# Attention scores as (64,32) tiles of the array, and another order of the first loads, in a fused attention and FFN kernel

## The chip, the cores and the metric

The kernel runs on one core of a Trainium2 chip. The metric is the device time of one execution in microseconds (us). TensorE is called PE, VectorE DVE, ScalarE ACT, GpSimd POOL and SyncE SP, as in the profile; PEld is PE's loading of weights.

## The reference

The inputs are q, k and v of 8 batches, 12 heads, 448 positions and 64 elements, two vectors g_q and g_k of 64, and the weights w1, w2 (768 x 1024), w3 (1024 x 1024) and w_out (1024 x 768), all in float32.

```python
q_n, k_n = rmsnorm(q, g_q), rmsnorm(k, g_k)      # x / sqrt(mean(x*x) + 1e-6) * g
scores = q_n @ k_n^T / sqrt(64)
attn = softmax(scores)
x = (attn @ v), as 3584 tokens x 768             # heads side by side
out = ((x @ w1) * (x @ w2)) @ w3 @ w_out
```

## The kernel before

**Units of work.** A quad is four heads of one batch, so there are 24 quads, three to a batch. The 448 positions stand as 112 partitions times J = 4. For each quad, q and k are loaded in float32 by SP (`load_qk`, L98; for quad 0 in two halves, k's on ACT's queue) and v in bfloat16 by POOL (`load_v`, L116).

**Preparation of a quad**, in two halves of two heads (pr = 0, 1): squares on ACT (`prep_sq`, L148), sums on DVE (`prep_red`, L163), the factor alpha = 1/rms by a logarithm and an exponential on ACT (`prep_alpha`, L170), three multiplications on DVE (`prep_scale`, L181): q by alpha, that by the product of both g vectors (`g_b`, L195), k by alpha. Then q and k are transposed to qkT, where the 64 elements of one head stand on partitions 0 to 63 and those of the other on 64 to 127: for quads 0 to 4 on PE, with a copy on DVE (`prep_pe_transpose`, L214), later by a DMA from SP (L210).

**Scores.** `qk_exp(i, g)` (L226) makes two groups of keys, jk, for one half of a quad. For each it issues two matmuls, one for each head, u = 0 and 1: 112 keys as weights, 64 rows, 448 queries moving. Both write one `sc` tile (one PSUM bank each), and one exponential on ACT takes both. The pool of `sc` has two buffers.

**The rest of attention.** `pv_set` (L248) runs three times for a quad: the sums of P over the keys (kind 0, weights of ones), and P times v in two halves. Four heads are four tiles of 32 columns of the array. ACT makes the reciprocal, DVE the product, into xT.

**FFN.** w3 and w_out are multiplied once to w34: 8 transposes of w3 (`w3_transpose`, L290) and 16 units of 8 matmuls (`w34_unit`, L298), 8 for each half nh of w_out's columns. LAG (L64) says how many units later the second half's units begin. `ffn1_a`, `ffn1_b` and `ffn2` (L323 to L374) do x·w1, x·w2 and the product with w34; each group of matmuls is cut in four tiles of 32 columns (`narrow`, L312).

**Order.** The order is written out by hand. A slot t = 4i + sl holds, on every engine in this sequence: loads of q and k that are due, `qk_exp(i, sl)`, one `pv_set` of the quad before (for sl below 3), up to four weight loads from the list wq, one or two pieces of w34 (W34_SLOTS, slots 1 to 13) or, later, up to two pieces of FFN, then the transposes and the other parts of preparation that are due. PREP_1 (L66) and PREP (L70) give, in slots before the quad's own, when each part is due; PREP_1 is for quad 1. What is left of FFN runs after the last slot. Engines work in their own order, so an instruction that waits holds what follows it on its engine.

**The start.** POOL first loads g_q and g_k, each copied to 112 partitions (L401, L402), and makes the identity; then a copy of one column of quad 0's k (`gate`, L410) holds POOL until that k has landed. After it come the loads of w_out's first half (nh = 0), four chunks of w3, v of quad 0, and w_out's second half. The rest of w3, v of quads 1 and 2, w1 and w2 follow from wq. SP is given q and k of quad 0, then of quad 1 (L408) and, in slot 0, of quad 2. PE warms up on 16 matmuls of zeros. DVE multiplies the two g tiles and scales them by 8 to g_b (L424, L425) between alpha and the first scaling.

Of the kernel before, what the change touches and what calls it, by code (L numbers as in the profile page):

```python
# [8 lines left out]
FP = mybir.dt.float32  # L9
BF = mybir.dt.bfloat16  # L10
MULT = mybir.AluOpType.mult
# [7 lines left out]
def kernel(  # L19
# [13 lines left out]
    nc = tc.nc  # L33

    B, H, S, D = q.shape
    NP = 112
    J = S // NP
# [23 lines left out]
    N_PE_T = 5  # L61
    N_SQ_ACT = 24
    W34_EV = "DA"
    LAG = 4  # L64
    SHIFT = [0, 0, 0, -1, -2, -3, -4]
    PREP_1 = {  # L66
        "sq0": -4, "red0": -4, "sq1": -4, "red1": -3, "alpha": -3,
        "sc0": -3, "t0": -2, "sc1": -2, "t1": -1,
    }
    PREP = {  # L70
        "load": -8, "sq0": -5, "red0": -5, "sq1": -4, "red1": -4, "alpha": -3,
        "sc0": -3, "t0": -2, "sc1": -2, "t1": -1,
# [6 lines left out]
    w_outs = const.tile([128, CF, DM], BF, name="w_outs")  # L79
    w3s = big_pool.tile([128, CF, DFF], BF, tag="big", name="w3s")  # L80
    w3T = big_pool.tile([128, CF, DFF], BF, tag="big", name="w3T")
    gq_b = const.tile([NP, D], FP, name="gq_b")
    gk_b = const.tile([NP, D], FP, name="gk_b")
    g_b = const.tile([NP, D], BF, name="g_b")
    ident = const.tile([128, 128], BF, name="ident")
    ones = const.tile([NP, HALF], BF, name="ones")
# [11 lines left out]
    def load_qk(i, split=1, k_eng=None):  # L98
        b, m = divmod(i, NQB)
        s = st[i]  # L100
        s["q"] = load_pool.tile([NP, HQ, J, D], FP, tag="q", name="q_sb")
        s["k"] = load_pool.tile([NP, HQ, J, D], FP, tag="k", name="k_sb")
        n = HQ // split
        for h0 in range(0, HQ, n):
            for t_sb, src, eng in (
                (s["q"], q, nc.sync),
                (s["k"], k, k_eng or nc.sync),
            ):
                eng.dma_start(
                    out=t_sb[:, h0 : h0 + n].rearrange("p h j d -> p h (j d)"),  # L110
                    in_=src[b, HQ * m + h0 : HQ * m + h0 + n].rearrange(
                        "h (p j) d -> p h (j d)", j=J
                    ),
                )

    def load_v(i):  # L116
        b, m = divmod(i, NQB)
        s = st[i]
        s["v"] = load_pool.tile([NP, HQ, J, D], BF, tag="v", name="v_sb", bufs=4)
        nc.gpsimd.dma_start(  # L120
            out=s["v"].rearrange("p h j d -> p h (j d)"),
            in_=v[b, HQ * m : HQ * (m + 1)].rearrange("h (p j) d -> p h (j d)", j=J),
        )
# [9 lines left out]
    def load_w3(c):  # L133
        nc.gpsimd.dma_start(
            out=w3s[:, c, :],
            in_=moe_w3.rearrange("(c p) f -> p c f", p=128)[:, c, :],
        )

    def load_wout(nh, c):
        nc.gpsimd.dma_start(  # L140
            out=w_outs[:, 4 * c : 4 * c + 4, nh * NH : (nh + 1) * NH],
            in_=moe_w_out.rearrange("(c p) n -> p c n", p=128)[
                :, 4 * c : 4 * c + 4, nh * NH : (nh + 1) * NH
            ],
        )


    def prep_sq(i, pr, on_act=False):  # L148
# [77 lines left out]
    def qk_exp(i, g):  # L226
        s = st[i]
        if g == 0:
            s["P"] = att_pool.tile([NP, HQ, J, S], BF, tag="P", name="P")
        pr, t = divmod(g, 2)  # L230
        qkT, P = s["qkT"], s["P"]
        for jk in (2 * t, 2 * t + 1):
            sc = sc_psum.tile([NP, 2, 512], FP, tag="sc", name="sc")
            for u in range(2):
                nc.tensor.matmul(  # L235
                    out=sc[:, u, 0:S],
                    lhsT=qkT[u * D : (u + 1) * D, pr, J + jk, :],
                    rhs=qkT[u * D : (u + 1) * D, pr, 0:J, :].rearrange(
                        "d j p -> d (j p)"
                    ),  # L240
                    start=True,
                    stop=True,
                )
            nc.scalar.activation(  # L244
                out=P[:, 2 * pr : 2 * pr + 2, jk, :], in_=sc[:, :, 0:S], func=AF.Exp
            )
# [151 lines left out]

    with tc.manual_schedule():

        nc.gpsimd.dma_start(out=gq_b, in_=g_q.unsqueeze(0).broadcast_to([NP, D]))  # L401
        nc.gpsimd.dma_start(out=gk_b, in_=g_k.unsqueeze(0).broadcast_to([NP, D]))  # L402
        nc.vector.memset(warm_t, 0.0)
        nc.vector.memset(eps_t, 64e-6)
        nc.vector.memset(ones, 1.0)
        load_qk(0, split=2, k_eng=nc.scalar)
        nc.scalar.preload_act_table_set("natural_log_exp_and_others")
        load_qk(1)  # L408
        make_identity(nc, ident)
        nc.gpsimd.tensor_copy(out=gate, in_=st[0]["k"][:, HQ - 1, 0, 0:1])  # L410
        load_wout(0, 0)
        load_wout(0, 1)
        for c in range(4):
            load_w3(c)
        load_v(0)
        load_wout(1, 0)
        load_wout(1, 1)
        warm(16)
        for pr in range(2):
            prep_sq(0, pr, on_act=True)  # L420
            prep_red(0, pr)
            prep_alpha(0, 2 * pr, 2 * pr + 2)
            if pr == 0:
                nc.vector.tensor_tensor(out=gq_b, in0=gq_b, in1=gk_b, op=MULT)  # L424
                nc.vector.tensor_scalar(  # L425
                    out=g_b, in0=gq_b, scalar1=8.0, scalar2=None, op0=MULT
                )
            prep_scale(0, pr, pe=True)
            if pr == 0:
                prep_pe_transpose(0, 0)  # L430

        wq = [lambda c=c: load_w3(c) for c in range(4, CF)]
        wq.insert(2, lambda: load_v(1))
        wq.append(lambda: load_v(2))
        for h in range(HQ):
            for half in range(2):
                for w, src in ((w1s, moe_w1), (w2s, moe_w2)):
                    wq.append(
                        lambda w=w, src=src, h=h, half=half: load_w12(w, src, h, half)
                    )  # L440
        wq.append(lambda: load_v(3))

        w34q = [lambda: w3_transpose(0), lambda: w3_transpose(1)]
        for fc in range(CF + LAG):
            if fc < CF:
                w34q.append(lambda fc=fc: w34_unit(fc, 0))
            if fc + 2 < CF:
                w34q.append(lambda fc=fc: w3_transpose(fc + 2))
            if fc >= LAG:
                w34q.append(lambda fc=fc: w34_unit(fc - LAG, 1))  # L450

        def prep_part(n, part):
            pe = n < N_PE_T
            if part[:2] == "sq":
                prep_sq(n, int(part[2]), on_act=n < N_SQ_ACT)
            elif part[:3] == "red":
                prep_red(n, int(part[3]))
            elif part == "alpha":
                prep_alpha(n)
            elif part[:2] == "sc":  # L460
                prep_scale(n, int(part[2]), pe=pe)
            elif pe:
                prep_pe_transpose(n, int(part[1]))


        agenda = {}
        for n in range(1, NQ):
            shift = SHIFT[min(n, len(SHIFT)) - 1]
            table = PREP_1 if n == 1 else PREP
            for part, rel in table.items():  # L470
                agenda.setdefault(max(0, 4 * n + rel + shift), []).append((n, part))

        for i in range(NQ + 1):
            for sl in range(4):
                t = 4 * i + sl
                mine = agenda.pop(t, [])
                for n, part in mine:
                    if part == "load":
                        load_qk(n)
                if i < NQ:  # L480
                    qk_exp(i, sl)
                if t == 0:
                    prep_pe_transpose(0, 1)
                seen = len(fillers)
                if i > 0 and sl < 3:
                    pv_set(i - 1, sl)
                fresh = fillers[seen:]
                if sl == 0 and 4 <= i + 1 < NQ:
                    load_v(i + 1)
                for _ in range(4):  # L490
                    if wq:
                        wq.pop(0)()
                if t in W34_SLOTS:
                    for _ in range(W34_SLOTS[t]):
                        if w34q:
                            w34q.pop(0)()
                elif not w34q:
                    left = (14 - t) % 12 + 1
                    old = len(fillers) - sum(1 for f in fillers if f in fresh)
                    fill(min(2, -(-old // left)))  # L500
                for n, part in mine:
                    if part[0] == "t":
                        prep_part(n, part)
                for n, part in mine:
                    if part[0] != "t" and part != "load":
                        prep_part(n, part)
        fill(len(fillers))
# [28 lines left out]
```

## Time and profile before

| | us |
|---|---|
| median of 13 runs | 392.55 |
| lowest, highest | 391.14, 393.98 |
| the profiled execution's own time | 391.63 |
| its span, first to last instruction | 389.9 |
| first scores (slot 0) start | 13.30 |
| first w3 transpose starts | 20.96 |
| first DMA of w_out is issued | 6.61 |

The profile is of one execution. A row of a group gives busy time and the mean length of one instruction; matmuls overlap, since the next one starts before the one before has left the array, so the distance between starts tells more than the length. In the timeline each row is a run of equal instructions: start, time until the last end, engine, line, names, and in brackets the idle time ahead of it with what ended it. The granted PE clock was full in the span but for the stretch from 11 to 25 us, where it was half.

### The profile page before, as it was taken

What the parts mean: (1) busy time and instruction counts of PE and PEld (TensorE: products, weight loads), DVE (VectorE), ACT (ScalarE), POOL (GpSimd) and SP (SyncE); (2) the same over time, 40 slices, a digit from 0 to 9 for tenths busy, and PEclk for the clock granted to TensorE, in tenths of its full rate; (3) what the DMA queues carried; (4) which work ended last, traced back from release to release, by engine and by line L of the source; (5) the groups of instructions that cost most, each with busy time, mean ns of one, the idle gap of its engine ahead of it and who ended that gap; (6) DMA issues with size and microseconds to landing.
All of it is one profiled execution on the core that took longest, in us unless ns stands there. A gap on an engine that the chain in (4) does not pass through costs nothing.

```text
span 389.9 us, 14802 instructions
## 1 busy us (share of the span) xinstructions
PE 372.3 (96%) x6688; PEld 193.3 (50%) x6688; DVE 242.2 (62%) x383; ACT 285.2 (73%) x467; POOL 35.4 (9%) x61
## 2 busy tenths in 40 slices
PE   5489999999999999999999999999999999999995
PEld 1155554544544455445544554445445555456563
DVE  1766766887767577567766766757776672234232
ACT  4559889998888885897899768888889857751210
POOL 5232440000000000000000000000000000000000
PEclk9579999999999999999999999999999999999999
DMA  8999999476994589675877479558955652003014
GB/s 186 226 236 237 222 227 180 69 148 141 217 190 88 114 168 208 127 162 95 189 174 151 86 221 204 76 109 199 205 92 122 119 141 27 3 12 114 2 26 141
DMA packets 78367, 55.08 MB, mean 141 GB/s; under 512 B 37824, under 2 KB 72160, under 8 KB 78304
## 3 DMA queue, kind: packets, MB, share of 16 engines
q1 hardware_dynamic: 61568, 41.30, 44.4%
q0 software_dynamic: 16256, 12.38, 22.4%
q8 instruction: 52, 0.85, 0.9%
q10 hardware_dynamic: 480, 0.46, 0.4%
q14 instruction: 11, 0.09, 0.1%
HBM read 46.72 MB, written 11.01 MB: 148 GB/s over the span
## 4 chain that ended last, share of the span: by engine, by line
PE 87%; DMA 8%; ACT 1%; DVE 1%; POOL 0%; issue 0%; ACTq 0%
PE pa L314 19%; PE po L314 19%; PE pb L314 19%; PE pv L259 15%; PE sc L235 12%; DMA w3s<-in_moe_w_dram 4%; PE wps L301 3%; DMA w_outs<-in_moe_w_out_dram 3%; DMA k_sb<-in_k_dram 1%; PE w3T_ps L293 1%; PE qkT_ps L220 0%; ACT P L244 0%; DVE qtmp L188 0%; ACT w34s L286 0%; DVE qks L201 0%; ACT sq L157 0%
## 5 line engine op out<-in xcount | busy, mean ns | idle before, releaser
L244 ACT ACTIVATE P<-sc 112x896 bf16<-112x896 f32 x192 | 165.5, 916 | 42.1 <-PE sc L235 42.1
L344 DVE TENSOR_TENSOR abT<-pb,a_sb 128x448 bf16<-128x448 f32 x64 | 40.0, 624 | 77.1 <-PE pb L314 56.7
L314 PE MATMUL pa<-xT,w1s 128*32 128x448 bf16 x1536 | 84.0, 353 | 0.0
L314 PE MATMUL pb<-xT,w2s 128*32 128x448 bf16 x1536 | 83.8, 352 | 0.0
L314 PE MATMUL po<-w34s,abT 128*32 128x384 bf16 x1792 | 77.9, 326 | 0.0
L166 DVE TENSOR_REDUCE ssq<-sq 112x16 f32<-112x1024 f32 x48 | 58.3, 1215 | 14.2 <-ACT sq L157 14.2
L314 PEld LDWEIGHTS <-abT 128*32 128x32 bf16 x1792 | 47.3, 97 | 27.6 <-issue 2.4
L235 PE MATMUL sc<-qkT 64*112 64x448 bf16 x384 | 57.4, 378 | 0.7 <-DVE qkT L223 0.7
L314 PEld LDWEIGHTS <-w2s 128*32 128x32 bf16 x1536 | 41.2, 97 | 31.4
L314 PEld LDWEIGHTS <-w1s 128*32 128x32 bf16 x1536 | 39.8, 96 | 34.0 <-issue 4.7
L331 ACT CAST a_sb<-pa 128x448 bf16<-128x448 f32 x64 | 34.0, 531 | 26.5 <-PE pa L314 26.5
L363 DVE COPY o_sb<-po 128x384 f32<-128x384 f32 x56 | 31.2, 557 | 31.5 <-PE po L314 31.5
L259 PE MATMUL pv<-P,v_sb 112*32 112x448 bf16 x768 | 45.1, 355 | 0.0
L120 POOL DMA_DIRECT2D v_sb<-in_v_dram x24 | 17.0, 709 | 237.6 <-PE pv L259 217.6
L188 DVE TENSOR_TENSOR qtmp<-q_sb,alpha 112x512 bf16<-112x512 f32 x48 | 32.7, 682 | 5.7 <-ACT alpha L177 5.7
L235 PEld LDWEIGHTS <-qkT 64*112 64x112 bf16 x384 | 17.5, 126 | 31.8 <-issue 29.4
L201 DVE TENSOR_TENSOR qks<-k_sb,alpha 112x512 bf16<-112x512 f32 x48 | 32.8, 684 | 0.0
L157 ACT ACTIVATE sq<-q_sb 112x512 f32<-112x512 f32 x48 | 30.5, 635 | 1.8 <-DMA q_sb<-in_q_dram 1.8
L275 DVE TENSOR_TENSOR xT<-pv,r 128x448 bf16<-128x448 f32 x48 | 29.6, 616 | 3.2 <-PE pv L259 3.2
L157 ACT ACTIVATE sq<-k_sb 112x512 f32<-112x512 f32 x48 | 30.0, 625 | 0.0
L259 PEld LDWEIGHTS <-v_sb 112*32 112x32 bf16 x768 | 16.2, 95 | 23.6 <-issue 15.1
L301 PE MATMUL wps<-w_outs,w3T 128*128 128x384 bf16 x128 | 23.4, 332 | 0.0
(36 smaller groups left out, 174.1 us busy)
## 6 DMA issues: line engine op xcount, KB each, us to landing
q_sb<-in_q_dram SPq DMA_DIRECT2D x23, 448.0 KB, 5.6
k_sb<-in_k_dram SPq DMA_DIRECT2D x23, 448.0 KB, 6.2
v_sb<-in_v_dram POOLq DMA_DIRECT2D x24, 224.0 KB, 4.7
out_dram<-o_sb SPq DMA_DIRECT2D x8, 336.0 KB, 4.0
out_dram<-o_sb SPq DMA_DIRECT2D x8, 288.0 KB, 3.4
w3s<-in_moe_w_dram POOLq DMA_DIRECT2D x8, 256.0 KB, 15.0
out_dram<-o_sb SPq DMA_DIRECT2D x8, 240.0 KB, 4.4
w_outs<-in_moe_w_out_dram POOLq DMA_DIRECT2D x4, 384.0 KB, 13.4
```

Of the source, the lines that this page charges most:

```text
L157: nc.scalar.activation(out=sq[:, t], in_=src[:, hs], func=AF.Square)
L166: nc.vector.tensor_reduce(out=s["ssq"][:, :, hs, :], in_=s.pop(("sq", pr)), axis=AX, op=ADD)
L188: nc.vector.tensor_tensor(out=qtmp.transpose([0, 2, 1, 3]), in0=s["q"][:, hs], in1=alpha[:, 0, hs].unsqueeze(3).broadcast_to([NP, 2, J, D] ...
L201: nc.vector.tensor_tensor(out=qks[:, 1].transpose([0, 2, 1, 3]), in0=s["k"][:, hs], in1=alpha[:, 1, hs].unsqueeze(3).broadcast_to([NP, 2, ...
L235: nc.tensor.matmul(out=sc[:, u, 0:S], lhsT=qkT[u * D : (u + 1) * D, pr, J + jk, :], rhs=qkT[u * D : (u + 1) * D, pr, 0:J, :].rearrange("d ...
L244: nc.scalar.activation(out=P[:, 2 * pr : 2 * pr + 2, jk, :], in_=sc[:, :, 0:S], func=AF.Exp)
L259: nc.tensor.matmul(out=ps[h * HALF : (h + 1) * HALF, :], lhsT=w, rhs=P[:, h, jk, :], start=(jk == 0), stop=(jk == J - 1), tile_position=(0 ...
L301: nc.tensor.matmul(out=ps[:, 0:NH], lhsT=w3T[:, gc, fc * 128 : (fc + 1) * 128], rhs=w_outs[:, gc, nh * NH : (nh + 1) * NH], start=(gc == 0 ...
L314: nc.tensor.matmul(out=ps[32 * h : 32 * h + 32, 0:n], lhsT=lhsT[:, 32 * h : 32 * h + 32], rhs=rhs, start=start, stop=stop, tile_position=( ...
L331: nc.scalar.copy(out=a_sb, in_=ps[:, 0:S])
L344: nc.vector.tensor_tensor(out=abT[bp][:, fi, odd * S : (odd + 1) * S], in0=ps[:, 0:S], in1=a_tiles.pop((b, fi)), op=MULT,)
L363: nc.vector.tensor_copy(out=o_sb[:, nh * NH : (nh + 1) * NH], in_=ps[:, 0:NH])
```

## The change

Six things are changed.

- The scores: each matmul with 112 keys as weights becomes four, with 32, 32, 32 and 16 keys, each at its own 32 columns of the array and the 64 rows of its head.
- The g vectors: each is loaded as one row of 64 by ACT's queue, after quad 0's k. DVE makes 8·g_q·g_k in one instruction, PE spreads it to 112 partitions (a matmul with a row of ones), and DVE copies it to g_b.
- The loads of weights: the gate on POOL is gone, so they are issued after the identity. Their order is another: w_out's second half (o1) comes after the last chunk of w3.
- Quad 1's q and k are loaded in slot 0 in place of ahead of it.
- Quad 1's preparation is due one slot later, part for part.
- LAG is 8 in place of 4: the units of w34 for w_out's second half come after all those for the first.

That five quads are transposed on PE (N_PE_T) is so in both.

```diff
-    LAG = 4
+    LAG = 8
+    LOADS_0 = ["o0", "w0", "w1", "w2", "v0", "w3", "w4"]
+    LOADS_1 = ["w5", "v1", "w6", "w7", "o1", "v2"]
+    GATE = None
+    QK1_AT = 0
-    PREP_1 = {
-        "sq0": -4, "red0": -4, "sq1": -4, "red1": -3, "alpha": -3,
-        "sc0": -3, "t0": -2, "sc1": -2, "t1": -1,
-    }
+    PREP_1 = {"sq0":-3,"red0":-3,"sq1":-3,"red1":-2,"alpha":-2,"sc0":-2,"t0":-1,"sc1":-1,"t1":0}
...
+    def load_any(x):
+        kind, a = x[0], int(x[1])
+        if kind == "o":
+            load_wout(a, 0)
+            load_wout(a, 1)
+        elif kind == "w":
+            load_w3(a)
+        else:
+            load_v(a)
...
             for u in range(2):
-                nc.tensor.matmul(
-                    out=sc[:, u, 0:S],
-                    lhsT=qkT[u * D : (u + 1) * D, pr, J + jk, :],
...
+                for c0 in range(0, NP, 32):
+                    c1 = min(c0 + 32, NP)
+                    nc.tensor.matmul(
+                        out=sc[c0:c1, u, 0:S],
+                        lhsT=qkT[u * D : (u + 1) * D, pr, J + jk, c0:c1],
+                        rhs=qkT[u * D : (u + 1) * D, pr, 0:J, :].rearrange(
+                            "d j p -> d (j p)"
+                        ),
+                        start=True,
+                        stop=True,
+                        tile_position=(u * D, c0),
+                    )
...
-        nc.gpsimd.dma_start(out=gq_b, in_=g_q.unsqueeze(0).broadcast_to([NP, D]))
-        nc.gpsimd.dma_start(out=gk_b, in_=g_k.unsqueeze(0).broadcast_to([NP, D]))
...
+        nc.vector.memset(ones_row, 1.0)
         load_qk(0, split=2, k_eng=nc.scalar)
+        nc.scalar.dma_start(out=g_row[:, 0], in_=g_q.unsqueeze(0))
+        nc.scalar.dma_start(out=g_row[:, 1], in_=g_k.unsqueeze(0))
         nc.scalar.preload_act_table_set("natural_log_exp_and_others")
-        load_qk(1)
+        if QK1_AT < 0:
+            load_qk(1)
         make_identity(nc, ident)
-        nc.gpsimd.tensor_copy(out=gate, in_=st[0]["k"][:, HQ - 1, 0, 0:1])
-        load_wout(0, 0)
-        load_wout(0, 1)
-        for c in range(4):
-            load_w3(c)
-        load_v(0)
-        load_wout(1, 0)
-        load_wout(1, 1)
+        if GATE is not None:
+            nc.gpsimd.tensor_copy(out=gate, in_=st[0][GATE[0]][:, GATE[1], 0, 0:1])
+        for x in LOADS_0:
+            load_any(x)
...
-                nc.vector.tensor_tensor(out=gq_b, in0=gq_b, in1=gk_b, op=MULT)
-                nc.vector.tensor_scalar(
-                    out=g_b, in0=gq_b, scalar1=8.0, scalar2=None, op0=MULT
-                )
+                nc.vector.scalar_tensor_tensor(
+                    out=gp_row, in0=g_row[:, 0], scalar=8.0, in1=g_row[:, 1],
+                    op0=MULT, op1=MULT,
+                )
+                g_ps = mm_psum.tile([NP, D], FP, tag="mm", name="g_ps")
+                nc.tensor.matmul(
+                    out=g_ps, lhsT=ones_row, rhs=gp_row, start=True, stop=True
+                )
+                nc.vector.tensor_copy(out=g_b, in_=g_ps)
...
-        wq = [lambda c=c: load_w3(c) for c in range(4, CF)]
-        wq.insert(2, lambda: load_v(1))
-        wq.append(lambda: load_v(2))
+        wq = [lambda x=x: load_any(x) for x in LOADS_1]
...
                 t = 4 * i + sl
+                if t == QK1_AT:
+                    load_qk(1)
```

More of the change, by code (lines that the diff above doesn't have):

```diff
@@ L81 @@
     w3T = big_pool.tile([128, CF, DFF], BF, tag="big", name="w3T")
-    gq_b = const.tile([NP, D], FP, name="gq_b")
-    gk_b = const.tile([NP, D], FP, name="gk_b")
+    g_row = const.tile([1, 2, D], FP, name="g_row")
+    gp_row = const.tile([1, D], BF, name="gp_row")
+    ones_row = const.tile([1, NP], BF, name="ones_row")
     g_b = const.tile([NP, D], BF, name="g_b")
@@ L234, in qk_exp @@
             for u in range(2):
-                nc.tensor.matmul(
-                    out=sc[:, u, 0:S],
-                    lhsT=qkT[u * D : (u + 1) * D, pr, J + jk, :],
[L238 to L242, printed above, removed]
-                )
+                for c0 in range(0, NP, 32):
[10 more added lines that the diff above has]
+                    )
             nc.scalar.activation(
```

## The prediction

> **What bounds the kernel now.** The page's busy shares come first, then the page's group of the scores. PE is the fullest engine by far, and the scores (L235) are the only tiled matmuls whose mean differs from that of others with as many columns.
>
> ```profile
> span 389.9 us, 14802 instructions
> PE 372.3 (96%) x6688; PEld 193.3 (50%) x6688; DVE 242.2 (62%) x383; ACT 285.2 (73%) x467; POOL 35.4 (9%) x61
> ...
> L314 PE MATMUL pb<-xT,w2s 128*32 128x448 bf16 x1536 | 83.8, 352 | 0.0
> ...
> L235 PE MATMUL sc<-qkT 64*112 64x448 bf16 x384 | 57.4, 378 | 0.7 <-DVE qkT L223 0.7
> ```
>
> A busy share doesn't say that PE streams all the time, so the timeline of PE is read next, by starts. Columns: start, length until the last end, instructions. First a stretch of the long middle:
>
> ```profile
> 211.03 1.31 PE L314 MATMUL pb<-xT,w2s 128*32 128x448 bf16 x24
> 212.26 0.59 PE L235 MATMUL sc<-qkT 64*112 64x448 bf16 x4
> 212.78 0.94 PE L259 MATMUL pv<-P,v_sb 112*32 112x448 bf16 x16
> 213.55 1.31 PE L314 MATMUL pa<-xT,w1s 128*32 128x448 bf16 x24
> ```
>
> Four 32-column tiles run side by side, so 24 matmuls are 6 sets and 16 are 4. From pv to pa is 0.77 us for 4 sets: 0.19 each, nothing lost at the seam. From pb to sc is 1.23 us where 6 sets need 1.14: 0.09 to 0.10 lost on the way in. From sc to pv is 0.52 us where 2 sets need 0.38: 0.14 lost. So a slot (one call of qk_exp) loses about 0.24 us around its scores and nothing else; PE has no other hole. Then the early stretch, where 128-column weights stand beside the scores:
>
> ```profile
> 54.06 0.56 PE L220 MATMUL qkT_ps<-ident,qks 112*128 112x112 bf16 x8
> 54.55 0.59 PE L235 MATMUL sc<-qkT 64*112 64x448 bf16 x4
> 55.06 2.77 PE L301 MATMUL wps<-w_outs,w3T 128*128 128x384 bf16 x16
> ```
>
> Transposes are 0.049 apart: 8 take 0.39, and sc starts at 0.49, again 0.10 late. sc to wps is 0.51, like sc to pv. The same price, whatever changes.
>
> Last the timeline of the start, all engines; brackets give idle time before and its releaser:
>
> ```profile
> 6.61 1.56 POOL L140 DMA_DIRECT2D w_outs<-in_moe_w_out_dram  x2
> 7.61 0.22 ACT L177 ACTIVATE alpha<-lnv 112x16 f32<-112x16 f32 x1
> 9.86 0.23 DVE L424 TENSOR_TENSOR gq_b<-gq_b,gk_b 112x64 f32<-112x64 f32 x1 [2.62 <-DMA gk_b<-in_g_k_dram]
> 10.23 0.68 DVE L188 TENSOR_TENSOR qtmp<-q_sb,alpha 112x512 bf16<-112x512 f32 x1
> 13.30 0.99 PE L235 MATMUL sc<-qkT 64*112 64x448 bf16 x4 [0.72 <-DVE qkT L223]
> 20.96 1.04 PE L293 MATMUL w3T_ps<-ident,w3s 128*128 128x128 bf16 x8 [2.69 <-DMA w3s<-in_moe_w_dram]
> 21.93 0.99 PE L235 MATMUL sc<-qkT 64*112 64x448 bf16 x4
> 29.41 0.59 PE L235 MATMUL sc<-qkT 64*112 64x448 bf16 x4
> ```
>
> The first scores wait for the g vectors, the third for the first w3 chunk. From 29.41 (slot 4) on, starts follow each other at stream time plus the losses above. The kernel is a start of some 27 us, then PE alone.
>
> **What the Trainium skill says.** TensorEngine Tiling (Array Packing), Key Properties: changing the tiling mode, not just the tile, drains TensorE, and modes are named by rows and columns. The trace agrees that 0.09 to 0.10 us goes at each change, but every change seen here changes columns as well (128 to 112, 112 to 32), so it shows no change of rows alone. TensorE: Matmul & The Clock Gate, Back-to-back issue gap: columns/2.4 + 2.5 ns, 189 for 448; the trace has 0.19. Same page, Packing small matmuls: tiles of one set start about 4 ns apart; no row of these views resolves it, so 4 is an estimate from that page. DMA: Bandwidth & Descriptors, Issuing engines are not separate DMA queues: all queues share 16 engines; in the trace their share is above 1.0 in every stretch from 2 to 66 us, so nothing is moved faster, only in another order.
>
> **The change part by part.**
>
> *Scores as (64,32) tiles.* 384 matmuls become 1536, in sets of 8. Price per slot now: entry 0.10, exit 0.09, and 0.05 of the 0.14 between sc and pv, which I put down to the first 112-column weight load (112/2.4 = 47 ns, an estimate). What the new form does: (a) still 64 rows beside 128, so by the skill both drains stay: 0.19, unchanged. (b) The exposed load falls to that of 32 columns; pv, which has such loads, takes 0.77 for 4 sets of 0.189, so 0.01: saves 0.035. (c) The last of 8 tiles starts some 24 ns after the first instead of 4: costs 0.02 at the exit. Net −0.013 us a slot. Of 96 slots, 93 are in the PE-bound part: −1.2 us. Bounds: all of the 0.24 gone (−22) on one side; on the other, a feed limit, below. 1152 more pairs of load and matmul are hidden under 189 ns sets as long as the queue in front of PE holds them.
>
> *g as one row.* Two 28 KB broadcasts on POOL's queue go (7.8 us to landing for gk), two rows of 256 B on ACT's queue, behind k's two transfers, come. ACT's table load is pushed back by two issues (0.48 each, from the 0.96 for two k issues) to about 4.0, still ahead of its first square at 4.84. DVE's wait ends at 9.86 now; alpha is done at 7.83. New chain: the row product (0.2, as L424), a 64-column matmul (0.3), a copy (0.25). The k halves land before 6.5, the rows with them or up to 2 us later: qtmp starts at 8.2 to 8.8 instead of 10.23. Slots 0 and 1 move by about −1.8.
>
> *Weight loads at once.* The gate at 6.49 and the two broadcasts (1.25 us of POOL) go; the first w_outs issue moves from 6.61 to about 1.9. q and k of quad 0 are issued at 0.74 to 1.69, ahead of it, so I cost the crowding at nothing; if they share alike, k's second half lands up to 1 us later, covered by the 2 us that DVE gains. On SP, quad 1's loads stand ahead of no new instruction, so moving their call costs nothing; q2 and k2 now wait for quad 0's first landings (some 2 us), and are not needed before slot 3. In bytes ahead of the first w3 chunk (four q/k loads of 0.46 MB at 240 GB/s, 7.7 us; two w_outs pieces and the chunk, about 5) it lands near 17.7 instead of 20.96: −3.2 for slot 2's scores. o1 goes behind w7; the later w3 chunks come earlier, and slot 5's wait for one (0.24 us) goes. o1 is needed from slot 9; by bytes it is there by 40, slot 9 stands near 43.
>
> *Quad 1's preparation one slot later (PREP_1), LAG 8.* This gives part back. Its squares, four of 0.52 on ACT, now stand behind exp of slot 1; quad 1's first scale follows in slot 2. I followed the in-order queues: exp of slot 1 at 16.3, squares to 20.2, exp of slot 2 to 21.9, copy of the first w3·w_out piece to 23.1, alpha at 23.7, DVE's three scales to 25.3, two copies (0.68 and 0.62) to 26.9, scores of slot 4 at 27.0 instead of 29.41: −2.4. Slot 4 then has the 8 transposes that slot 3 had: +0.4. With slot 5's wait gone: −2.3 when the PE-bound part begins. Bounds: if the chunk lands no earlier, slot 4 stands where it did (0); if the half clock of 11 to 25 us ends sooner, −4.5. LAG only reorders equal pieces: 0. What is late next after slot 4 is PE itself.
>
> Sum against the profiled run (391.63, span 389.9): −2.3 − 1.2 = −3.5, so 388.1. That run stands 0.9 under the median of 392.55; from the median, 389.0.
>
> **The rivals.**
>
> *Drain gone.* If the array drains for columns and not for rows, the scores join their neighbours: 93 slots times 0.22 to 0.23 is −21. ACT then comes near: in a quad of FFN work (scores at 202.05 and, four slots on, 215.92) PE falls from 13.9 to 12.9 us, while ACT needs 8 exps of 0.86, 4 squares, 4 casts and small ones, 12.6. I take 3 us back for that, and add the start: about 372. For it: no row-only change in the trace. Against: the skill names modes by both, and the same loss stands at every change.
>
> *Feed limit (slower).* Nothing in the trace shows load-matmul pairs fed faster than po's 256 in 10.4 us, 40.7 ns each. If that is the feed's own pace and nothing is stored ahead, a group of 16 pairs takes 0.65 us instead of 0.42: +0.22 a slot, +21 in 93 slots, less 2.3: about 411. It decides from where 16 pairs cost 3.5/93 = 0.04 us above today's group, near 29 ns a pair. Against: sets of four start together, so pairs are stored.
>
> *The start gives nothing* (the chunk no earlier, or preparation later eats it): −1.2 or a little over, 391.5 to 393.
>
> **How the numbers follow.** Likeliest 52%: 386.5 to 391, at 389.0. Drain gone 28%: 368 to 378. No gain at the start 9%: mostly within 0.2%, which is about what measuring this kernel can tell from no change (391.8 to 393.3). Feed limit and the like 11%: 394 to 412. Faster is 52 + 28 = 80, same 9, slower 11. The range 368 to 392 leaves out the slower cases and a little of the third; the likeliest's own is 386.5 to 391.
>
> **What would show it.** Scores to pv 0.50 us and pb to sc 1.23: drains stayed. Around 0.39 and 1.14: gone. Above 0.6: feed. Slot 4's scores at 27; qtmp at 8.2 to 8.8; first w3 transpose near 17.7. A DMA wait on w_outs or w3s after slot 4, or idle PE <- ACT in the middle, would make me wrong.

## The result, and the profile after

| | before | after |
|---|---|---|
| median (us) | 392.45 of 48 runs | 387.78 of 11 runs |
| lowest, highest | 391.14, 394.67 | 386.83, 391.55 |
| profiled execution, its span | 391.63, 389.9 | 387.92, 386.1 |

The ratio of after to before is 0.9889, with a 95% interval of 0.987 to 0.9908: 4.4 us less (the two medians of the table differ by 4.7). The forecast was 3.5 less. First the page of the kernel after: span, busy time, the group of the scores, and the queue by which instructions are fetched (packets, MB, share of the DMA engines).

```profile
span 386.1 us, 17109 instructions
PE 371.9 (96%) x7841; PEld 189.1 (49%) x7841; DVE 242.6 (63%) x384; ACT 285.4 (74%) x467; POOL 34.1 (9%) x58
...
q8 instruction: 61, 1.00, 1.2%
...
L249 PE MATMUL sc<-qkT 64*32 64x448 bf16 (+1 forms) x1536 | 56.1, 360 | 1.9 <-DVE qkT L235 1.5
```

PE is busy as long as before, with 1153 more pairs of load and matmul (1152 for the scores, one for g). The busy share says nothing about the gain; the instruction queue, 52 packets before, will matter below. Next the timeline of PE in the kernel after, in the same long middle as in the prediction.

```profile
211.13 1.31 PE L329 MATMUL pb<-xT,w2s 128*32 128x448 bf16 x24
212.37 0.57 PE L249 MATMUL sc<-qkT 64*32 64x448 bf16 x16
212.87 0.94 PE L274 MATMUL pv<-P,v_sb 112*32 112x448 bf16 x16
```

Scores follow pb by 1.24 us (1.23 before) and pv follows the scores by 0.50 (0.52 before). All the drains are still there. The start moved instead. Timeline of the kernel after, all engines:

```profile
1.45 1.64 POOL L142 DMA_DIRECT2D w_outs<-in_moe_w_out_dram  x2
8.00 0.21 DVE L437 SCALAR_TENSOR_TENSOR gp_row<-g_row 1x64 bf16<-1x64 f32 x1 [0.90 <-DMA g_row<-in_g_k_dram]
8.63 0.68 DVE L200 TENSOR_TENSOR qtmp<-q_sb,alpha 112x512 bf16<-112x512 f32 x1
11.70 0.94 PE L249 MATMUL sc<-qkT 64*32 64x448 bf16 x16 [0.72 <-DVE qkT L235]
16.56 1.03 PE L308 MATMUL w3T_ps<-ident,w3s 128*128 128x128 bf16 x8
25.66 0.57 PE L249 MATMUL sc<-qkT 64*32 64x448 bf16 x16 [0.76 <-DVE qkT L235]
```

DVE's first scaling (qtmp) comes 1.6 us sooner, the first w3 transpose comes 4.4 us sooner (20.96 before), and slot 4 stands 3.75 us sooner (29.41 before).

How the 3.8 us between the two spans add up, by the starts of the scores in the two timelines: at slot 6 after is 3.71 us ahead (32.49 against 36.20). By slot 95 it is 4.17 ahead (341.63 against 345.80), so 89 slots brought 0.46. From there to the end 0.4 is lost: the last output has landed 4.2 us sooner, but SP then looks at the landings of the last outputs in another order, with seven of them after the one that landed last.

89 slots at 16 ns each (0.252 us lost around the scores before, 0.236 after) should have brought 1.4, not 0.46. Nearly all of the rest is in two holes, places where PE starts nothing and the trace names nothing that it waits for. The first of them is here (timeline of after):

```profile
144.68 1.30 PE L329 MATMUL po<-w34s,abT 128*32 128x384 bf16 x25
146.29 1.00 PE L329 MATMUL po<-w34s,abT 128*32 128x384 bf16 x20 [0.31 <-issue]
```

The bracket counts from the modelled end of the last matmul; from the last start before it to 146.29 it is 0.64 us where 0.15 is usual, and a second such distance, of 0.56 where 0.18 is usual, begins at 151.65. Together 0.87 us too much. PE waits for no engine and no load there ("issue"). The trace of before has no such place.

### The profile page after: what moved, and what is told of

Its sections match the earlier page's. It is cut to its first block, busy times and chain, and to the rows that moved or that the text cites. A ratio compares the mean times of both kernels' runs of the same rounds, so it can differ in the third digit from the quotient of the medians.

```text
span 386.1 us, 17109 instructions
## 1 busy us (share of the span) xinstructions
PE 371.9 (96%) x7841; PEld 189.1 (49%) x7841; DVE 242.6 (63%) x384; ACT 285.4 (74%) x467; POOL 34.1 (9%) x58
## 4 chain that ended last, share of the span: by engine, by line
PE 90%; DVE 3%; ACT 3%; DMA 1%; issue 1%; ACTq 0%; DVEq 0%
PE pa L329 19%; PE po L329 19%; PE pb L329 19%; PE pv L274 16%; PE sc L249 12%; PE wps L316 4%; DMA g_row<-in_g_k_dram 1%; ACT P L259 1%; PE qkT_ps L232 1%; DVE qtmp L200 1%; ACT sq L169 1%; PE w3T_ps L308 1%; DVE qks L213 1%; DVE qks L207 1%; ACT w34s L301 0%
## 5 line engine op out<-in xcount | busy, mean ns | idle before, releaser
L249 PE MATMUL sc<-qkT 64*32 64x448 bf16 (+1 forms) x1536 | 56.1, 360 | 1.9 <-DVE qkT L235 1.5
L249 PEld LDWEIGHTS <-qkT 64*32 64x32 bf16 (+1 forms) x1536 | 13.3, 87 | 34.1 <-issue 30.9
L274 PE MATMUL pv<-P,ones 112*32 112x448 bf16 x384 | 22.7, 355 | 0.2 <-issue 0.2
```

The costliest lines, as they stand in the source:

```text
L249: nc.tensor.matmul(out=sc[c0:c1, u, 0:S], lhsT=qkT[u * D : (u + 1) * D, pr, J + jk, c0:c1], rhs=qkT[u * D : (u + 1) * D, pr, 0:J, :].rearr ...
L274: nc.tensor.matmul(out=ps[h * HALF : (h + 1) * HALF, :], lhsT=w, rhs=P[:, h, jk, :], start=(jk == 0), stop=(jk == J - 1), tile_position=(0 ...
```

## Experiments

Theory at the outset: the drains stay, tiles are worth little, and the start carries the gain. Rivals: the tiles carry it; or parts of the start are worth nothing, or cost.

### The tiles alone, and the rest alone

`tiles_only` is the kernel before with the new score tiles; `rest_only` is the kernel after with the old ones.

```diff
-                nc.tensor.matmul(out=sc[:, u, 0:S], lhsT=qkT[u*D:(u+1)*D, pr, J+jk, :], ...
+                for c0 in range(0, NP, 32):
+                    c1 = min(c0 + 32, NP)
+                    nc.tensor.matmul(out=sc[c0:c1, u, 0:S], ..., tile_position=(u * D, c0))
```

> The kernel before with nothing changed but the scores as (64,32) tiles. My theory: both drains stay, only the exposed weight load shrinks, so sc to pv is 0.50 us in place of 0.52, a slot gains 0.013 to 0.02 us, and the whole gains 1 to 2 us (ratio 0.995 to 0.998). The start is as before: first w3 transpose at 21, slot 4 at 29.4. Rival (the tiles carry most of the change): a ratio near 0.989.

> The changed kernel with the scores as they were, two matmuls of 112 keys for each group. My theory: the start carries most of the change, so slot 4 stands near 25.7 as in the changed kernel, the middle has 0.24 us lost a slot again, and the whole gains 2.5 to 3.5 us against before (ratio 0.991 to 0.994). Rival (the tiles carry it): a ratio within 0.998 to 1.002.

Measured: `tiles_only` 392.04, ratio 1.0001 (0.9971 to 1.003); `rest_only` 389.03, ratio 0.9928 (0.9906 to 0.9951). The start carries the gain: 0.72% of the 1.11%, though the intervals of `rest_only` and after just touch. The tiles, whose distances are as in after, gave nothing measurable alone; the interval leaves room for about 1 us either way. The timeline of `tiles_only` shows two places where PE stands:

```profile
34.12 0.62 PE L296 MATMUL w3T_ps<-ident,w3s 128*128 128x128 bf16 x8 [0.98 <-DMA w3s<-in_moe_w_dram]
...
148.16 1.47 PE L317 MATMUL po<-w34s,abT 128*32 128x384 bf16 x29
150.90 1.32 PE L317 MATMUL po<-w34s,abT 128*32 128x384 bf16 x28 [1.28 <-issue]
```

Slot 5 waits about a microsecond for a chunk of w3, where before waited 0.24. Slot 4 came 0.93 sooner than in before (28.48), because the first chunk of w3 happened to land sooner, and most of that head start goes here: slot 6 is only 0.23 ahead (35.97). The tiles' own saving, some 1.4 us, goes into the hole, of 1.44 us.

### Fewer instructions, the same tiles of rows

`tiles64` is after, `tiles64_only` is before, both with keys in pieces of 64 and 48 in place of 32, 32, 32 and 16. That is half the pairs for the scores; the instruction queue then has 55 packets in place of 61.

```diff
-                for c0 in range(0, NP, 32):
-                    c1 = min(c0 + 32, NP)
+                for c0 in range(0, NP, 64):
+                    c1 = min(c0 + 64, NP)
```

> The changed kernel with the scores cut at 64 keys: tiles of 64 and 48 columns, four matmuls for a group. By my terms the exposed load is that of 64 columns (27 ns) and the last of four tiles starts about 10 ns after the first: from sc to pv 0.189 + 0.027 + 0.093 + 0.189 + 0.010, 0.51 us, between 0.52 of the kernel before and 0.50 of the changed one; the entry is unchanged. If the load's width had no part in it, 0.50 as in the changed kernel.

> The kernel before with the scores cut at 64 keys (tiles of 64 and 48 columns), nothing else. The profiled run of the 32-column tiles alone had a hole of 1.4 us at 149 us in which PE waited for nothing that the trace shows, while the run with 64-key tiles and the new start had none. Theory (more instructions are fetched late and that eats the gain): this form saves the same 0.016 us a slot with 384 more pairs in place of 1152, has no hole, and is 1 to 1.5 us faster than before (ratio 0.996 to 0.998). Rival (the gain is eaten elsewhere, at the start, where w3 is waited for): ratio 0.999 to 1.001 and no hole.

Measured: `tiles64` 386.97 in its one run, span 385.2 (after 386.1). `tiles64_only` 390.63, ratio 0.9965 (0.9947 to 0.9983), and faster than before by more than the interval, which the 32-key form was not. Its profile waits for w3 at slot 5 as well, 1.73 us, and slot 6 comes 1.03 later than in before (37.23); from slot 6 to slot 95 it needs 308.20 us where before needs 309.61, so the whole saving of 1.4 us arrives. The expectation set a late fetch against a wait for w3; both are seen, but only the hole takes what the tiles save. Timeline of `tiles64`:

```profile
211.44 0.57 PE L249 MATMUL sc<-qkT 64*64 64x448 bf16 x8
211.94 0.94 PE L274 MATMUL pv<-P,v_sb 112*32 112x448 bf16 x16
```

0.50 us, as with 32 keys: from one set of scores to the next 210 ns instead of 200, from the last to pv 289 instead of 299. No hole in either profile. From slot 4 to slot 95 `tiles64` needs 315.10 us and after 315.97; the difference is the 0.87 of after's holes. So both forms cost the same around the scores.

All fourteen profiles put side by side: holes of 0.2 to 1.4 us stand in five of the seven with 61 packets of instructions (after, `tiles_only`, `gate_back`, `warm_after`, `lag4`; not in `prep_early` and `g_wide`), and in none of the seven with 52 to 55. In the DMA records such packets (1.00 MB in 61, so 16 KB each) mostly come 4 to 7 us apart in the kernel after. Before its first hole the gap was longer, 8.9 us: the transfer was done at 144.91 and PE went on at 146.29. Before the second the gap was the usual 5.1, but the transfer was slow: it began at 148.79, was done at 150.67, and PE went on at 152.21. In `tiles_only` it came after a gap of 10.0, was done at 149.57, and PE went on at 150.90. Counting smaller ones, these five profiles have nine such stops, and `tiles64` has one of 0.06 us; every one of the ten ends 1.3 to 1.5 us after a packet has landed. That is what running out of instructions would look like. No run changes the fetch by itself, so this cause is inferred, not shown.

### What a drain costs

`same_mode` is after with the scores as tiles of 128 rows and 32 columns, the shape of their FFN neighbours. It leaves out the separation of the two heads: each matmul sums over both, one bank is written, and the exponential reads it twice. Half of the pairs, the same stream time (two sets of 448 columns), the same work on ACT.

```diff
-            for u in range(2):
-                for c0 in range(0, NP, 32):
-                    ... lhsT=qkT[u*D:(u+1)*D, pr, J+jk, c0:c1], tile_position=(u * D, c0)
+            for c0 in range(0, NP, 32):
+                ... lhsT=qkT[:, pr, J+jk, c0:c1], tile_position=(0, c0)
...
-                in_=sc[:, :, 0:S]
+                in_=sc[:, 0:1, 0:S].broadcast_to([NP, 2, S])
```

> The changed kernel with each group of scores as four tiles of 128 rows and 32 columns: one contraction over both heads' rows, so the scores are the sum of the two heads' and one bank is written and read twice by the exponential. The separation of the two heads is left out; the number of sets, of exponentials and everything else is kept. If the 0.19 us a slot is the price of going from 128 to 64 rows and back: pb to sc 1.14, sc to pv 0.39, and the whole gains up to 93 times 0.21, 20 us, less what ACT takes back (I put 3 us). If the loss belongs to the scores themselves (their waits, their two banks): no change against the changed kernel.

Measured: 367.89, ratio 0.9385 (0.9359 to 0.9411), some 20 us below after. Timeline of `same_mode`:

```profile
179.35 1.33 PE L326 MATMUL pb<-xT,w2s 128*32 128x448 bf16 x24
180.49 0.58 PE L248 MATMUL sc<-qkT 128*32 128x448 bf16 x8
180.87 0.96 PE L271 MATMUL pv<-P,ones 112*32 112x448 bf16 x16
```

From pb to scores 1.14, from scores to pv 0.38: what 6 and 2 sets stream, nothing lost. So going from 128 rows to scores of 64 rows, at 32 columns on both sides, costs 0.10 us on the way in, and the way back 0.09 (299 ns where 189 are streamed, of which some 0.02 is the stagger of eight tiles). Tiles of 112 rows (pv) beside 128 cost nothing.

The number of pairs plays no part in this: `tiles64` has as few, and the drains of after. One rival is not told apart by a run: `same_mode` also writes one bank for each group where after writes two, and no run keeps the two banks and changes only the rows. Against the banks speaks that the same price stands where one bank is written and only the columns change, here from 32 to 128 (timeline of `same_mode`):

```profile
49.58 0.56 PE L248 MATMUL sc<-qkT 128*32 128x448 bf16 x8
50.07 2.77 PE L313 MATMUL wps<-w_outs,w3T 128*128 128x384 bf16 x16
```

The distance is 0.49 us where the two sets need 0.38. The Trainium skill's sentence that a change of mode drains the array (TensorEngine Tiling (Array Packing), Key Properties) therefore fits a change of rows too, which the trace of before could not show apart; it gives no price, and here it is 0.2 us for a visit. From slot 4 to slot 95 `same_mode` is 20.1 us shorter than after. That is 80 slots of FFN at 0.235, 10 slots of w34 at half of it (their neighbours have 128 columns, so a change is left), and 0.87 of holes: 20.9. ACT takes back no more than the 0.8 between the two sums: PE waits for it nowhere in this stretch.

### The g vectors

`g_wide` is after with the two old broadcasts back on POOL's queue; nothing else is old.

```diff
+        nc.gpsimd.dma_start(out=gq_b, in_=g_q.unsqueeze(0).broadcast_to([NP, D]))
+        nc.gpsimd.dma_start(out=gk_b, in_=g_k.unsqueeze(0).broadcast_to([NP, D]))
-        nc.scalar.dma_start(out=g_row[:, 0], in_=g_q.unsqueeze(0))
-        nc.scalar.dma_start(out=g_row[:, 1], in_=g_k.unsqueeze(0))
```

> The changed kernel with g_q and g_k loaded to 112 partitions on POOL's queue as before, ahead of the weights, still with no gate. By my terms qtmp starts at about 10.2 in place of 8.63 and POOL's loads 1.25 us later; slot 2 waits for w3 or not, the preparation of slot 3 is the later one: slot 4 moves by 1 to 1.6 us (to 26.7 to 27.3) and the whole to 388.5 to 389.3. Rival (the wait for w3 covers it): slot 4 moves by less than 0.5.

Measured: 390.07, ratio 0.994 (0.9918 to 0.9962), 2.0 us above after by the ratios (2.3 by the medians) and more than was expected. Timeline of `g_wide`:

```profile
2.72 0.57 SPq L110 DMA_DIRECT2D q_sb<-in_q_dram  x1
10.19 0.23 DVE L435 TENSOR_TENSOR gq_b<-gq_b,gk_b 112x64 f32<-112x64 f32 x1 [3.42 <-DMA gk_b<-in_g_k_dram]
19.65 1.03 PE L307 MATMUL w3T_ps<-ident,w3s 128*128 128x128 bf16 x8 [1.08 <-DMA w3s<-in_moe_w_dram]
29.06 0.57 PE L248 MATMUL sc<-qkT 64*32 64x448 bf16 x16 [0.76 <-DVE qkT L234]
```

DVE waits for g until 10.19, as costed. But the first w3 transpose also moves, from 16.56 to 19.65, though w_out and w3 are issued at 3.06, only 1.6 us later than in after. Its releaser is the DMA of w3, so the weights land later. Two things delay them. The first is seen on SP's queue. In after, quad 2's q is issued here:

```profile
4.98 0.31 SPq L111 DMA_DIRECT2D q_sb<-in_q_dram  x1
```

It comes at 4.98, after a landing of quad 0, with the two g rows on ACT's queue, and at 2.72 without them. The prediction had this wait ("q2 and k2 now wait for quad 0's first landings") and put it at nothing, since they are not needed before slot 3. It is worth something: 0.9 MB of q and k are issued behind the first weights instead of ahead.

The second is the broadcasts themselves. A line of the DMA page of before, cut to 4 to 10 us, gives the packets, the MB and the share of the 16 engines' time of POOL's queue, which holds only the two broadcasts there:

```profile
q0 software_dynamic: 64, 0.06, 26.2%
```

For 0.06 MB they hold a quarter of the engines' time. In these 6 us all queues together moved 205 to 236 GB/s in the five profiles with the broadcasts (227 in before, 205 in `g_wide`), and 240 to 282 in the nine without (249 in after, 282 in `gate_back`).

In `g_wide` the broadcasts also hold POOL: its fifth chunk of w3 is issued only at 10.37, after gk has landed. How much each of these is worth was not told apart, and the half clock lasted to 25.88 in this profile (below), so its 3.4 us at slot 4 are not all the edit's.

### The gate

`gate_back` is after with POOL held, as before, until a half of quad 0's k has landed.

```diff
-    GATE = None
+    GATE = ("k", 3)
```

> The changed kernel with the gate back: POOL's loads wait until quad 0's k has landed. Theory (the early issue of the weights carries most of the gain at the start): the first w3 transpose goes from 16.56 to 19 to 21 us, slot 4 from 25.66 to 28 to 29, and the whole loses 2 to 3 us (390 to 391). Rival (the g row carries it): slot 4 stays within 0.5 us and the whole within 0.7 us.

Measured: 390.06 (387.43 to 391.54 in 10 runs), ratio 0.9929 (0.99 to 0.9959). By the ratios the gate costs 1.6 us (2.3 by the medians), but the interval overlaps that of after. The profiled execution took only 387.44, and its timeline says something else:

```profile
17.48 1.03 PE L308 MATMUL w3T_ps<-ident,w3s 128*128 128x128 bf16 x8 [0.74 <-DMA w3s<-in_moe_w_dram]
```

The weights are issued 5 us later than in after (6.42), and yet the first transpose comes 0.9 later, and slot 4 0.35 later (26.01). All of q and k still lands ahead of the weights here, but sooner: quad 2's at 11.12 and 12.77, where before has 14.23 and 16.34. With the broadcasts gone from the DMA engines, the queues are done earlier. So in the profile it is the g rows more than the early issue that bring w3 in: 3.5 of the 4.4 us at the first transpose, if before's 20.96 is taken as it is (four profiles with the old start have it between 19.23 and 20.96). The profiled run is one of the kernel's three shortest, and the spread of both kernels is wide; what the gate costs in the median stays open.

### Quad 1's preparation

`prep_early` is after with quad 1's parts due one slot sooner, as before.

```diff
-    PREP_1 = {"sq0":-3,"red0":-3,"sq1":-3,"red1":-2,"alpha":-2,"sc0":-2,"t0":-1,"sc1":-1,"t1":0}
+    PREP_1 = {"sq0":-4,"red0":-4,"sq1":-4,"red1":-3,"alpha":-3,"sc0":-3,"t0":-2,"sc1":-2,"t1":-1}
```

> The changed kernel with quad 1's preparation due where it was before, one slot earlier. My prediction said that the later place gives time back. If so, quad 1's squares run on ACT between the first two exponentials, alpha comes about 2 us sooner, slot 4's scores start at 24.0 to 24.7 in place of 25.66, and the whole gains 1 to 1.5 us on the changed kernel (386.3 to 386.8 us). Rival (something else is late for slot 4: the first w3 pieces or the copies on DVE; or the squares now hold slot 1's exponential): slot 4 at 25.5 or later and 387.5 to 389 us.

Measured: 388.39, ratio 0.9892 (0.9867 to 0.9917): the same as after. Timeline of `prep_early`:

```profile
16.80 1.72 ACT L259 ACTIVATE P<-sc 112x896 bf16<-112x896 f32 x2
17.76 0.57 PE L249 MATMUL sc<-qkT 64*32 64x448 bf16 x8 [0.31 <-ACT P L259]
19.90 2.77 PE L316 MATMUL wps<-w_outs,w3T 128*128 128x384 bf16 x8
26.07 0.57 PE L249 MATMUL sc<-qkT 64*32 64x448 bf16 x16
```

The exponentials of slot 1 stand behind the squares and start at 16.80 instead of 16.33, and slot 2's scores wait for them. Alpha is done at 19.9 instead of 22.7, but slot 4 comes at 26.07 (25.66 in after) and slot 5 at 29.29 (29.27). The w34 unit at 19.90 runs at half clock, 2.77 us, where after's took 1.56, so part of the gain may hide there; and slot 4 differs as much between profiles with the same start (see the last section). That the later place gives something back is not shown.

### LAG

`lag4` is after with LAG 4.

> The changed kernel with LAG 4 as before. I costed LAG at nothing, as a mere order of equal pieces. With LAG 4 the first piece that needs w_out's second half (o1) stands in slot 7, near 38 us in the changed kernel, where o1 lands at about 38 to 40: if so, PE waits up to 2.5 us there and the whole is 1.5 to 2.5 us slower than the changed kernel (389 to 390): LAG 8 is then not free of effect but what lets o1 be late. If o1 is there in time: within 0.5 us of the changed kernel.

Measured: 389.39 (388.0 to 391.51), ratio 0.9934 (0.991 to 0.9958), 1.6 us above after by the medians; the two intervals just fail to meet. Timeline of `lag4`:

```profile
39.43 0.81 PE L316 MATMUL wps<-w_outs,w3T 128*128 128x384 bf16 x4 [0.99 <-DMA w_outs<-in_moe_w_out_dram]
```

With LAG 4 the units of o1, w_out's second half, begin in slot 7, and o1 is now the last of the weights. From start to start PE stands 1.16 us too long. LAG 8 is what lets o1 be late. (This profile also has a hole of 0.94 us, at 107.8.)

### The clock

In the profiles of before and after PE's granted clock is half for a stretch of the start. `warm_after` and `warm_before` put matmuls of zeros into the idle times of the start, whose results nobody reads.

```diff
+    def stay_warm(n):
+        ps = mm_psum.tile([128, 512], FP, tag="mm", name="stay_ps")
+        for _ in range(n):
+            nc.tensor.matmul(out=ps, lhsT=warm_t[:, 0:128], rhs=warm_t, start=True, stop=True)
```

> The changed kernel with matmuls of zeros put into PE's idle stretches of the start (2 more ahead of the g matmul, 6 after it, 3 after the first transposes, 8 ahead of the second), so that its clock is not halved; nothing else is changed. The profiled changed kernel had the half clock for 10.2 us, the kernel before for 13.7, and the changed kernel's times fall in two bunches, near 387 and near 389. Theory (the length of the half clock, not the change, decides between them, and accounts for what I had not forecast): the clock stays full or nearly so, slot 4's scores start at 24.2 to 25.2 in place of 25.66, and the times are at 385.5 to 386.7 with less spread. Rival (ACT and DVE set the start, the clock is covered): slot 4 within 0.3 us of 25.66 and 387 to 388.

> The kernel before with matmuls of zeros in PE's idle stretches of the start (20 more at the beginning, 3 and 8 around the first scores). Theory: the first w3 transpose still waits for its chunk to 20 to 21 us, but what follows it up to slot 4 runs at the full clock: slot 4 at 27.5 to 28.7 in place of 29.41, and 1 to 2 us in the whole. If the half clock is covered here by the wait for w3: within 0.5 us of before.

Measured: `warm_after` 388.33, ratio 0.9904 (0.987 to 0.9938); `warm_before` 392.36, ratio 1.0011 (0.9993 to 1.0029). In `warm_after` the clock is full throughout and slot 4 comes at 24.80, 0.86 sooner than in after, but this profile has two holes of 0.90 together, and the median is not better. In `warm_before` slot 4 comes 2.2 us sooner (27.25), though 1.7 of that stands already at the first w3 transpose (19.23), whose chunk landed sooner in this profile. And then, in its timeline:

```profile
33.62 0.90 PE L293 MATMUL w3T_ps<-ident,w3s 128*128 128x128 bf16 x8 [1.67 <-DMA w3s<-in_moe_w_dram]
34.31 2.76 PE L301 MATMUL wps<-w_outs,w3T 128*128 128x384 bf16 x8
```

PE waits for w3, the clock halves again for 3.4 us, and slot 6 starts at 37.01 (36.20 before). The start of before is bound by the landing of w3 at slot 5: what PE gains ahead of it is given back, as with `tiles_only`. In the profile of after PE waits for no w3 at slot 5, so there a gain can stay.

### Together

`combo` is after with 64-key tiles, quad 1's earlier preparation, the g rows on SP's queue, and matmuls of zeros.

> A version that may beat both: the changed kernel with 64-key tiles, quad 1's preparation one slot earlier, the g rows on SP's queue between quad 0's q and quad 1's, and matmuls of zeros in PE's idle stretches of the start. By my terms: the g rows are there 0.75 to 0.9 us sooner (qtmp at about 7.8), full clock 1 to 1.5 us, the earlier preparation up to 1 us once PE is not at half clock: slot 4 at 22.5 to 24 in place of 25.66, and 384.5 to 386 us. If ACT and DVE, in order, set the start: slot 4 at 24.5 or later and 386 to 387.

Measured: 387.59 (386.72 to 388.57), ratio 0.988 (0.9848 to 0.9912): within the interval of after. Scores of slot 0 start at 10.49 instead of 11.70, but those of slot 2 wait until 17.78 for a copy on DVE and for ACT. PE stands idle for 2.2 us there, the clock is half from 19.14 to 22.55 in spite of the zeros, the first w34 unit takes 2.76 us, and slot 4 is back at 25.56. How much the order on DVE and ACT and how much the clock is worth was not told apart. No version clearly beats the kernel after.

## Why the prediction was right, and where it was not

**Drains: right.** The likeliest case said that both drains stay, that the load shrinks by 0.035 and that the stagger of eight tiles costs 0.02, net 0.013 us a slot. Measured: entry 292 ns (293 before), set to set 200 (233), exit 299 (282): 0.033 gained, 0.017 lost, net 0.016. The last of eight tiles starts 22 ns after the first, 3.1 ns from tile to tile; the estimate of 4 from the Trainium skill's page (TensorE: Matmul & The Clock Gate, Packing small matmuls) was good. One reading was not exact: that PE has no other hole. In before as in after it waits 0.6 us for DVE once, where the last transposes on PE stand (near 67 us in before).

**Drain gone: fell, but its price was near.** It did not happen. `same_mode` puts its value at 20 us, so 368 with the new start, against the 372 that the rival named. The 3 us that it let ACT take back were not taken; but it counted 93 slots at full price, where the ten slots with w34 save half.

**Feed limit: in the forecast form wrong, in a mild form there.** Groups of 16 pairs take 0.50 us, far from 0.65, so single pairs are not paced. The holes, if they are the fetching of instructions, are a feed limit in another place: of 1.4 us of tile gain, 0.9 is lost in the profile of after. The prediction named the queue in front of PE, and not what fills it.

**The g row: the time right, the worth too small.** qtmp starts at 8.63 (8.2 to 8.8 forecast); with the same loads it starts at 9.28 in `rest_only` and 9.36 in `lag4`, so hitting the range was partly luck. Its side effects, quad 2's loads held back and the DMA engines freed of the broadcasts, were costed at nothing, and they move the weights.

**Weight loads: better than forecast.** First w3 transpose 16.56 (17.7 forecast). The prediction gave this to the early issue; `gate_back` and `g_wide` say that in the profiles more of it comes with the g rows. The step that failed is "nothing is moved faster, only in another order": it took a share above 1.0 as engines that can't move more, but a share counts the time of packets, and between 4 and 10 us the kernel after moved 249 GB/s where before moved 227.

**The start's term: the one that was mis-sized.** Forecast for slot 4: 27.0, or −2.4; measured 25.66, −3.75. With slot 5's wait gone, −2.3 when the PE-bound part begins; measured at slot 6, −3.71. The working holds up to the exponentials of slot 2 (to 21.9 forecast, some 0.2 sooner measured). It fails at "copy of the first w3·w_out piece to 23.1": that copy is done at 22.1, mostly because the eight matmuls of the piece took 1.56 us and not the 2.8 of a half clock (with 2.8 the copy would be done near 22.7, by the piece's start at 19.44 and the 0.50 of the copy). The prediction let the half clock last to 24.8 as in the profile of before. Columns of the next two rows: stretch, length, busy time of PE, PEld, DVE, ACT and POOL, granted clock, DMA share, GB/s. Before:

```profile
20.00:25.00 5.00, 4.04 (x25) 2.57 (x26) 2.31 (x3) 1.34 (x4) 1.76 (x4) 0.52 1.14 242
```

After:

```profile
20.00:25.00 5.00, 4.24 (x47) 2.24 (x44) 4.32 (x8) 4.97 (x10) 1.50 (x2) 1.00 1.17 247
```

Half in one, full in the other. The bound that the prediction gave for a clock that recovers sooner, −4.5, covers what came. No run shows that the change itself ends the half clock sooner: in `prep_early`, whose loads are those of after, it lasted to 23.23.

**LAG "0": wrong by itself.** With o1 late, LAG 4 waits 1.16 us. The prediction let o1 be late because it is needed only from slot 9; that is so with LAG 8, while with LAG 4 it is slot 7. It then gave LAG itself nothing; only together do the two cost nothing.

**The sum** was −3.5 against the profiled run, and between the two profiles −3.8 came: 1.4 more from the start and 0.2 more from the tiles than forecast, but 0.9 lost in holes and 0.4 at the end, both unforeseen. That the sum came so near is partly luck, since these errors cancel.

## What to carry to other kernels

Price a change of tile shape by the distance between starts on both sides of it, and test it once with a shape that removes the change altogether: here that showed 20 us in the drains. The 32-key tiles leave those as they are; their 1.4 us come from the shorter distance between the two sets. Cutting a matmul in four multiplies instructions; take the coarsest cut that has the effect (with 64 keys the distances added up to the same as with 32), and look for PE idle on "issue" in the middle. At the start, a load that is moved or added shifts what the queues hold ahead of others: ask of every DMA which later ones it lets go first, and which it holds.

## What the runs showed of the hardware

- From tiles of 128 rows to the scores' 64, at 32 columns on both sides, 0.10 us is lost on the way in and 0.09 on the way out, and nothing is when the scores have 128 rows (and write one bank in place of two). From 32 to 128 columns with 128 rows on both sides 0.10 is lost as well. 112 rows beside 128 cost nothing.
- Two broadcasts of 28 KB each, to 112 partitions, held 26% of the 16 DMA engines' time for 6 us.
- Between the two sets of scores the distance is 11, 21 and 44 ns longer than the stream for tiles of 32, 64 and 112 columns, 0.3 to 0.4 ns a column; that this is the load is an inference, as the number of tiles in a set changes along. The Trainium skill (TensorE: Matmul & The Clock Gate, LDWEIGHTS) prices a whole load at columns/1.2 ns, 0.83 a column: less than half of it is seen in the open.
- PE stops for 0.2 to 1.4 us with nothing to wait for that the trace names, in five of seven profiles with 61 packets of instructions and in none of seven with 52 to 55; every stop ends 1.3 to 1.5 us after such a packet has landed.
- The half clock at the start lasted 6.8, 10.2 or 13.7 us, two to four times 3.41: 13.7 in before, 10.2 in after, and 6.8 in `lag4`, whose start is that of after; with the zeros of `combo` it lasted 3.4. The same page (What's actually happening) says that the clock is decided in free-running windows of 3413 ns, which agrees.
- Profiles with the loads and preparation of after have slot 4 at 25.66 (after), 25.67 (`tiles64`), 26.20 (`lag4`), 26.33 (`rest_only`) and 25.04 (`same_mode`), as qtmp came sooner or later: from it to slot 4 are 16.8 to 17.1 us in all five. In `warm_after`, without a half clock, slot 4 is at 24.80, 16.5 us after qtmp. So a difference of a microsecond at the start need not come from an edit.
